# A searched order of steps, loads, casts and copies replaced by another: one q/k group exchanged by DMA, four in quadrants, ten casts on VectorE and not 16

## The chip, the cores and the metric

The kernel runs on one core of a Trainium2 chip. The metric is device time in microseconds (us) of one execution; lower is better. Engines are named as in the profile: PE (TensorE), ACT (ScalarE), DVE (VectorE), POOL (GpSimd), and SP (SyncE), which issues nearly all DMAs.

## What is computed

Sigmoid attention over 8 batches, 12 heads, 448 positions and head size 64, followed by a token-mixing MLP whose mixing weights are computed from its own input. All inputs and the output are float32.

```python
def _attn_ref(q, k, v):
    S = q.shape[2]
    scale = 1.0 / np.sqrt(q.shape[-1])
    scores = scale * np.matmul(q, k.transpose(0, 1, 3, 2)) - np.log(S)
    attn = 1.0 / (1.0 + np.exp(-scores))
    return np.matmul(attn, v).astype(np.float32)

def _moe_ref(x, w_q, w_k, w_out):
    d_hyper = w_q.shape[1]
    wq = x @ w_q
    wk = x @ w_k
    scale = 1.0 / np.sqrt(d_hyper)
    W_tok = scale * np.einsum('bsd,btd->bst', wq, wk)
    mixed = np.einsum('bst,btd->bsd', W_tok, x)
    return (np.maximum(mixed, 0.0) @ w_out).astype(np.float32)
```

Between the two, the heads are put side by side: x is 8 x 448 x 768. There is no softmax, so no row sums: each score goes through a sigmoid by itself. The mixing is done as wq times (wk transposed times x), so that the 448 x 448 matrix W_tok is never built.

## The kernel before

**Groups.** Four heads of one batch are a group; there are 24 groups, three to a batch (a batch is called a unit, u). Each group has seven blocks of 64 keys. q, k and v of a group are loaded as float32 by one DMA each (`load1`, 448 KB) into one of six buffers `ld`, cast to bf16 (`cast1`), and q and k are brought into the tile `qk` with the head size on the partitions (`tr`). `scores` multiplies one block of keys with all queries of four heads: four 64x64 matmuls (L303), then one sigmoid over 128x896 on ACT (L308). `values` (L321) adds up seven blocks of attention times v; after the seventh, the sum is copied to `xt` (L330).

**MLP of a unit.** x is turned around by `tr_x` (L344 in whole 128x128 blocks, L361 in 64x64), and projected by `mlp_wqk` (L400, or L387 in four 64x64 tiles, whose two halves are then added at L394 and L395). `mlp_wkn` turns wk, `mlp_tmp` (L431) or `mlp_tmp_tiled` (L447, L451, L452) makes wk times x, and `mlp_mix` (L471, L483) multiplies with wq, with the relu in the eviction (L457 on ACT, L459 on DVE). The output product of two units together (a window w) is `out_pair` (L516), `out_halves` (L556) or `out_chunk` (L600), with evictions at L525, L561, L562 and L633 and stores issued by SP.

**How q and k are turned** differs from group to group, by the letter of the group in PLAN:

- q/k: a plain cast, 28 transposes of 64x64 each on PE (L212) into PSUM, and one copy to `qk` (L291). a/b: the same with 7 transposes of 128x128 (L220, L286).
- c/d: a cast that also rearranges (L188), six copies of 32 partitions on POOL (`arrange`: L157, L160, L163), and two DVE transposes in blocks of 32x32 (L259), one by c and one by d. Nothing of it is on PE.
- r, s, z: the rearranging cast, two DVE transposes by r (L252), and `quadrants` on DVE (L228): two of 32 partitions by s, two by z. No `arrange`.
- e, f, g: the rearranging cast; e and f each make two DVE transposes, one into `qk` and one into the tile `mv`; g (`move`) has SP issue four DMAs which copy quarters of `mv` over quarters of `qk`. No `arrange`. Before uses no e, f, g.

**The order is a string.** `PLAN` has one letter for each piece of work, and the loop over PLAN at L812 issues it: S a score step, P a values step, W or L one of the six projection steps of a unit (W in one matmul, L in four tiles), x or X or Y one transposition of a third of x (x in 64x64 blocks), N, U or T, M and O or I the later MLP steps, C two DMAs that copy rows of w_out to other partitions, F and E matmuls on zeros that compute nothing. A lower-case p, o, m, i, l, t, u or y puts the eviction that the step ends with on ACT instead of DVE; only the step that ends a sum has one. All engines get their instructions in the order of PLAN, and each engine runs its own in that order, with semaphores where it needs another's result.

**Loads and casts** follow `ORDER`. SP issues loads in this order; a load waits until the buffer used six loads before it has been cast (`pump_loads`). A name without a dot is cast on POOL, one with a dot on DVE (`cast_one`), at the first score step that is at least nine steps behind its load. So a cast that is late holds back the load six places later, and everything behind that on SP.

PSUM is eight banks in four pairs: a score step, an open sum, a transposition each hold a pair or half of one until evicted.

Of the kernel before, what the change touches and what calls it, by code (L numbers as in the profile page):

```python
# [17 lines left out]
def kernel(  # L18
# [101 lines left out]
    def xt(u, j):  # L120
# [4 lines left out]


    PLAN = (
        "SSSFFFFKSqSFFSSkFFSPPSFPpSPPPSSSqkPPPSPPSpPSaSbSPPPSSXPSPPSr"
        "XSPSSsWWSSzWWWXSPWSppPSPNPPSqSkSUSXSMSpppSPMSppPSqkSPSPpPSXS"
        "PpPSWWSWcWSMSXdSWWPSPPSpNPpSPqSkSSUxSMSppSPPpSpPSoOSMCSooqSk"  # L130
        "SOOCMSpPPScpppSPSodOSSoXSSOLLLSLcLLSppPSPppPSSdoOSOSCxNCScOS"
        "USdPrSPpPSPpPpspSpPpSpSoPSXoSMzSooSLLLxSLLLSpPPSpPPScPSOXSSd"
        "OooSpCMpSPppPSPSoNMSCYOxSppPSPSocoPdSpPSoOSxScUdSLLLSLLLSppp"
        "cPSPPPSoOSdMSoOSXSMSprPPSppPSPoSoSoomszxoOcSOSOSoOSdNoSOSUSP"
        "pSMpPPppPPPSSPpcdLLLLSLLppooxmmoOScooSSoOOSONSoSOPdpSPPpSpoS"
        "POSOoSToSOoSOPSPPcSPPpPomMOmoxOSLLSLLdLLSooSoSOSoOScNoSOPSPp"
        "SPPPSoodSPoSOSoSOxSOSxoPppSTSppPpPpPPmpppmmWWWWYWWyIxNIiitii"
        "IMiIMmIIiOOoOooOOooOOoOoo"
    )
    PLAN = "".join(PLAN)  # L140
    KIND = ["a"] + [t for t in PLAN if t in "qacer"]
# [540 lines left out]
    for n in range(7):  # L682
# [1 line left out]


    ORDER = (
# [5 lines left out]
    )  # L692
    BY = {"s": [], "v": []}
    for x in ORDER.split():
# [219 lines left out]
```

## Time and profile before

| | |
|---|---|
| three runs | 187.12 us median (186.6 to 187.13) |
| the profiled execution | 188.48 us, of which the span from first to last instruction 186.7 |
| sigmoids on ACT (L308) | 168, the first at 6.2 us, the last at 162.1; 926 ns each in the mean, 141.2 us busy in all |
| granted PE clock | 0.995 in the mean |
| DMA | 48.52 MB, mean 260 GB/s |
| copies within SBUF (w_out) | 12 DMAs of 96 KB, 5.6 to 8.4 us from issue to landing, median 7.1 |

The sigmoids are the clock of the kernel: 0.8 us from one to the next where nothing holds them up, one for each S in PLAN. Matmuls are pipelined: a row's mean (357 ns at L303) is the time of one from start to end, and four of them take 0.19 us of the engine where they follow one another. A row of the timeline gives start, duration, engine, line, operation and tiles, the number of instructions merged into it, and in brackets how long the engine was idle before it and what ended that.

### The profile page before, as it was taken

Reading aid. Unit: us, or ns where it says so; the run is one execution under the profiler, and the core shown is the slowest. Engines: PE = TensorE matmul, PEld = TensorE weight load, DVE = VectorE, ACT = ScalarE, POOL = GpSimd, SP = SyncE. Lnnn points to the kernel's source line nnn. Section 1 sums busy time; section 2 is a strip of 40 time slices with the busy share of each in tenths; the row PEclk is TensorE's granted clock in tenths of the full one; section 3 lists DMA queues with packets and bytes.
Section 4 is the critical chain, followed back from the end, with each engine's and each line's share of the span. In section 5 each row is a group of like instructions: output and inputs, shape, how many; then the busy total and the mean of one; then the engine's idle time right before and its main releaser. Section 6 shows DMA issues by size and latency. Waiting matters only on the chain.

```text
span 186.7 us, 8457 instructions
## 1 busy us (share of the span) xinstructions
PE 175.0 (94%) x3612; PEld 116.9 (63%) x3612; DVE 139.3 (75%) x222; ACT 163.8 (88%) x208; POOL 113.5 (61%) x158
## 2 busy tenths in 40 slices
PE   7798998998799999999999999999999999999990
PEld 7344545553455554655565768778888888869660
DVE  3334697798778989998899899976476865697830
ACT  4799999998979999999999999998998899976320
POOL 1458788994759999799977796997059800000000
PEclk9999999999999999999999999999999999999997
DMA  5999999998989999799999797886677353421596
GB/s 169 366 384 379 322 374 362 346 320 283 353 303 307 311 364 329 244 272 356 375 325 320 235 301 285 255 271 215 165 191 230 86 135 89 115 61 41 141 241 176
DMA packets 26086, 48.52 MB, mean 260 GB/s; under 512 B 3968, under 2 KB 19968, under 8 KB 26048
## 3 DMA queue, kind: packets, MB, share of 16 engines
q1 hardware_dynamic: 25888, 47.79, 79.2%
q8 instruction: 28, 0.46, 1.0%
q10 hardware_dynamic: 160, 0.20, 0.4%
q14 instruction: 10, 0.08, 0.2%
HBM read 35.78 MB, written 11.01 MB: 251 GB/s over the span
## 4 chain that ended last, share of the span: by engine, by line
PE 67%; ACT 11%; DVE 5%; DMA 5%; issue 5%; POOL 3%; SPq 1%; DVEq 0%; ACTq 0%; POOLq 0%
PE banks L516 15%; PE banks L303 13%; PE banks L321 12%; PE banks L600 11%; ACT at L308 10%; DMA ld<-in_q_dram 3%; PE banks L556 3%; PE banks L387 2%; DMA ld<-in_v_dram 2%; PE banks L431 2%; PE banks L344 2%; PE banks L471 2%; DVE qk L228 1%; PE banks L361 1%; DVE xn L349 1%
## 5 line engine op out<-in xcount | busy, mean ns | idle before, releaser
L308 ACT ACTIVATE at<-banks 128x896 bf16<-128x896 f32 x168 | 141.2, 926 | 5.3 <-PE banks L303 4.5
L303 PE MATMUL banks<-qk 64*64 64x448 bf16 x672 | 63.9, 357 | 1.4 <-ACT at L308 0.3
L321 PE MATMUL banks<-at,v 64*64 64x448 bf16 x672 | 46.4, 351 | 0.4 <-ACT at L308 0.2
L303 PEld LDWEIGHTS <-qk 64*64 64x64 bf16 x672 | 26.5, 105 | 18.2 <-issue 8.7
L516 PE MATMUL banks<-wout,mx 64*64 64x384 bf16 x672 | 35.9, 323 | 0.3 <-issue 0.3
L321 PEld LDWEIGHTS <-v 64*64 64x64 bf16 x672 | 24.1, 106 | 9.7 <-issue 3.7
L330 DVE CAST xt<-banks 128x896 bf16<-128x896 f32 x20 | 21.7, 1087 | 8.3 <-PE banks L321 8.0
L188 POOL CAST qk<-ld 128x896 bf16<-128x896 f32 x21 | 25.2, 1213 | 4.3 <-issue 1.4
L516 PEld LDWEIGHTS <-mx 64*64 64x64 bf16 x672 | 24.5, 107 | 4.1 <-issue 0.7
L600 PE MATMUL banks<-wout,mx 128*128 128x384 bf16 (+1 forms) x138 | 24.7, 320 | 0.1
L198 POOL CAST v<-ld 128x896 bf16<-128x896 f32 x23 | 21.6, 949 | 2.4 <-DMA ld<-in_v_dram 1.6
L157 POOL COPY swap<-qk 32x448 uint32<-32x448 uint32 x26 | 15.1, 582 | 11.4 <-DVE qk L188 10.0
L459 DVE TENSOR_SCALAR mx<-banks 128x1024 bf16<-128x1024 f32 (+2 forms) x19 | 18.6, 989 | 2.3 <-PE banks L483 0.9
L600 PEld LDWEIGHTS <-mx 128*128 128x128 bf16 x138 | 12.0, 97 | 11.3 <-issue 5.0
L163 POOL COPY qk<-swap 32x448 uint32<-32x448 uint32 x26 | 15.6, 600 | 1.5
L259 DVE STREAM_TRANSPOSE qk<-qk 128x448 f32<-128x448 f32 x26 | 16.3, 631 | 0.0
L525 DVE COPY o<-banks 128x768 f32<-128x768 f32 x11 | 10.5, 957 | 7.0 <-PE banks L516 5.2
L160 POOL COPY qk<-qk 32x448 uint32<-32x448 uint32 x26 | 14.5, 556 | 1.5
L374 DVE COPY xn<-banks 128x1024 bf16<-128x1024 bf16 (+1 forms) x12 | 7.7, 645 | 2.3 <-PE banks L361 1.9
L457 ACT ACTIVATE mx<-banks 128x448 bf16<-128x448 f32 (+1 forms) x11 | 8.0, 768 | 1.4 <-PE banks L483 0.8
L349 DVE COPY xn<-banks 128x1024 bf16<-128x1024 bf16 (+1 forms) x11 | 7.3, 660 | 2.1 <-PE banks L344 1.3
L188 DVE CAST qk<-ld 128x896 bf16<-128x896 f32 x11 | 7.9, 750 | 0.1
(95 smaller groups left out, 210.7 us busy)
## 6 DMA issues: line engine op xcount, KB each, us to landing
ld<-in_q_dram SPq DMA_DIRECT2D x24, 448.0 KB, 6.1
ld<-in_v_dram SPq DMA_DIRECT2D x24, 448.0 KB, 6.1
ld<-in_k_dram SPq DMA_DIRECT2D x23, 448.0 KB, 5.8
out_dram<-o SPq DMA_DIRECT2D x42, 192.0 KB, 4.0
ld<-in_moe_w_out_dram SPq DMA_DIRECT2D x6, 384.0 KB, 5.9
out_dram<-ld SPq DMA_DIRECT2D x11, 192.0 KB, 2.8
wout<-wout SPq DMA_DIRECT2D x12, 96.0 KB, 7.1
out_dram<-ld SPq DMA_DIRECT2D x4, 96.0 KB, 2.5
```

Source lines behind the costliest of these rows:

```text
L157: eng.tensor_copy(out=z[lo], in_=w[hi, 0])
L163: eng.tensor_copy(out=w[lo, 1], in_=z[lo])
L188: COPY[e](out=f[:, :, "qk".index(nm)].rearrange("p e i d y -> p e y i d"), in_=ld.pop((nm, n)).rearrange("p (y i e d) -> p e y i d", y=2, ...
L198: COPY[e](out=t16.rearrange("p i b d -> p b i d"), in_=ld.pop((nm, n)).rearrange("p b (i d) -> p b i d", i=NI),)
L259: nc.vector.transpose(out=qk[n][:, t].rearrange("p t i n -> p (t i n)").bitcast(F32), in_=w)
L303: nc.tensor.matmul(sc[HALF[h], g, 0:S], qk[n][HALF[g], h, 1, i, :], qk[n][HALF[g], h, 0].rearrange("p i n -> p (i n)"), start=True, stop=True,
L308: nc.scalar.activation(at, sc[:, :, 0:S], ACTF.Sigmoid, bias=attn_bias, scale=attn_scale)
L321: nc.tensor.matmul(ps[HALF[g], h, 0:S], ld["v16", n][HALF[h], i, g, :], ats[n, i][HALF[h], g, :], start=(i == 0), stop=(i == NI - 1),)
L330: COPY[eng](out=xt(u, j)[:, :, 0:S], in_=ps[:, :, 0:S])
L459: nc.vector.tensor_scalar(dst, ps, moe_scale, 0.0, ALU.mult, ALU.max)
L516: nc.tensor.matmul(ps[HALF[x], y, 0:NB], mx[HALF[y], u, b, 64 * (i - 3 * y) : 64 * (i - 3 * y) + 64], wout16[HALF[y], slot(y, b), x * NB : ...
L600: nc.tensor.matmul(ps, mxs[w][:, 2 * S * c + m * P : 2 * S * c + (m + 1) * P], wout16[:, c, w0:w1], start=(c == 0), stop=(c == NC - 1),)
```

## The change

Only the two strings change; every letter in the new ones is already served by the code.

```diff
     PLAN = (
-        "SSSFFFFKSqSFFSSkFFSPPSFPpSPPPSSSqkPPPSPPSpPSaSbSPPPSSXPSPPSr"
-        "XSPSSsWWSSzWWWXSPWSppPSPNPPSqSkSUSXSMSpppSPMSppPSqkSPSPpPSXS"
-        "PpPSWWSWcWSMSXdSWWPSPPSpNPpSPqSkSSUxSMSppSPPpSpPSoOSMCSooqSk"
-        "SOOCMSpPPScpppSPSodOSSoXSSOLLLSLcLLSppPSPppPSSdoOSOSCxNCScOS"
-        "USdPrSPpPSPpPpspSpPpSpSoPSXoSMzSooSLLLxSLLLSpPPSpPPScPSOXSSd"
-        "OooSpCMpSPppPSPSoNMSCYOxSppPSPSocoPdSpPSoOSxScUdSLLLSLLLSppp"
-        "cPSPPPSoOSdMSoOSXSMSprPPSppPSPoSoSoomszxoOcSOSOSoOSdNoSOSUSP"
-        "pSMpPPppPPPSSPpcdLLLLSLLppooxmmoOScooSSoOOSONSoSOPdpSPPpSpoS"
-        "POSOoSToSOoSOPSPPcSPPpPomMOmoxOSLLSLLdLLSooSoSOSoOScNoSOPSPp"
-        "SPPPSoodSPoSOSoSOxSOSxoPppSTSppPpPpPPmpppmmWWWWYWWyIxNIiitii"
-        "IMiIMmIIiOOoOooOOooOOoOoo"
+        "SSSFFFFKESqSSFFjSFFSpSPPpSPPqSPSSkppSPSpPPSPSabSXSrESpSPpppS"
+        "XpPSSSSsWXWWWSpWSzWPSpPpSNPPSSSabSUSXSMSSPppqkSPPSPPPSPPSpMp"
+        "SpSPSWXcSSWWWWWSdPpppNSMSPSPPSFXSxSqkSUSppSMPPSPPPSOoMSSOOSq"
+        "kSooSPPrSMPCpPSpPCSooSsSSozXOLSLLLSLLCcPSPppSPPPSOSdOSOSCNxS"
+        "cOSUSPppSSdprpPPsPpSpPPSPSOPSXoSMSOoLCSLzxCSLLLLSppPSPppcSPS"
+        "odXSSoOOSMSppppSpcPPSONxSMYOSdSpppSPoopSpPSOOSxScUdSLLLSLLLS"
+        "pPPcSpPPSPoSodSMoSOSXmMPpSppSrPpOSosPSoPoozoSxSOOSOcSONSOdOS"
+        "SUpSPPPeSMpppllfllPPSpPllpSpOPgOSNOOSSOoxSoOSOSOmMOtopScPppp"
+        "SSPPoomodOSSoOSPOSOpSPPPSpPmOOSMOSOLLSLcdLSLoLSoSoOSSoONcoxd"
+        "SopPxPSPPPSPOSOxSoSoTOSOSoSOPpPSPPxSpppPpmpmpPPLmLLxLLLyiiiN"
+        "IIuiIMiMimIIIOoOOooOOOoOoOooo"
     )
...
     ORDER = (
-        "q1 .k1 v0 v1 q2 k2 k3 q3 v2 q4 k4 w0 v3 q5 v4 q6 k5 q7 w5 k6 v5 "
-        "q8 k7 .w4 .k8 k9 v6 w3 v7 .q9 q10 v8 w6 .k10 w2 w1 q11 .v9 v10 "
-        "k11 .k12 .q12 v11 .q13 k13 v12 v13 q14 v14 k14 v15 q15 k15 .q16 "
-        "v16 k16 .k17 .q17 q18 v17 v18 q19 k18 k19 k20 .k21 v19 .k22 q20 "
-        ".k23 q21 .q22 v20 q23 v21 v22 v23 "
+        "q1 .k1 v0 q2 k2 v1 k3 q3 v2 k4 q4 w0 v3 q5 .q6 k5 q7 v4 k6 w2 "
+        ".k7 v5 v6 w5 .w6 k8 w3 q8 k9 q9 v7 v8 w1 w4 v9 k10 q10 k11 q11 "
+        "v10 q12 k12 .k13 q13 v11 v12 q14 k14 q15 v13 .q16 k15 v14 v15 "
+        "v16 k16 .k17 .q17 k18 k19 v17 q18 q19 q20 k20 k21 v18 k22 .k23 "
+        "q21 v19 v20 .q22 v21 q23 v22 v23 "
     )
```

Counted out, by what the letters issue:

- Group 5 is turned by a/b, not q/k. Group 10 by r, s, z, not c/d. Group 20 by e, f, g, not c/d. All others stay as they were (r, s, z: 4, 13, 18; c/d: 7, 11, 12, 14 to 17, 19, 21 to 23).
- 25 rearranging casts on POOL, not 21; 36 plain casts of q, k and v, not 34; six of w in both. On DVE seven rearranging casts, not 11; two plain, not four; one of w in both (w6, not w4).
- 11 `arrange` on POOL, not 13, six copies each.
- The last unit's projection in four tiles (L), not one (W); its U in the untiled form. One x in 64x64 blocks more, one whole less.
- Before the last score step ACT has two evictions of `out_chunk` more, one of `out_pair` more, one each of the partial sums at L394 and L451 more, one of `mlp_mix` less, one of `values` less. Behind it two values steps less and one x less on PE.
- Two E added; nine F in both, one of them now near step 52.

The rest is where each letter stands. The counts of S, P, W and L together, x, N, U, M and O are the same.

More of the change, by code (lines that the diff above doesn't have):

```diff
@@ L127 @@
     PLAN = (
-        "SSSFFFFKSqSFFSSkFFSPPSFPpSPPPSSSqkPPPSPPSpPSaSbSPPPSSXPSPPSr"
-        "XSPSSsWWSSzWWWXSPWSppPSPNPPSqSkSUSXSMSpppSPMSppPSqkSPSPpPSXS"
-        "PpPSWWSWcWSMSXdSWWPSPPSpNPpSPqSkSSUxSMSppSPPpSpPSoOSMCSooqSk"
-        "SOOCMSpPPScpppSPSodOSSoXSSOLLLSLcLLSppPSPppPSSdoOSOSCxNCScOS"
-        "USdPrSPpPSPpPpspSpPpSpSoPSXoSMzSooSLLLxSLLLSpPPSpPPScPSOXSSd"
-        "OooSpCMpSPppPSPSoNMSCYOxSppPSPSocoPdSpPSoOSxScUdSLLLSLLLSppp"
-        "cPSPPPSoOSdMSoOSXSMSprPPSppPSPoSoSoomszxoOcSOSOSoOSdNoSOSUSP"
-        "pSMpPPppPPPSSPpcdLLLLSLLppooxmmoOScooSSoOOSONSoSOPdpSPPpSpoS"
-        "POSOoSToSOoSOPSPPcSPPpPomMOmoxOSLLSLLdLLSooSoSOSoOScNoSOPSPp"
-        "SPPPSoodSPoSOSoSOxSOSxoPppSTSppPpPpPPmpppmmWWWWYWWyIxNIiitii"
-        "IMiIMmIIiOOoOooOOooOOoOoo"
+        "SSSFFFFKESqSSFFjSFFSpSPPpSPPqSPSSkppSPSpPPSPSabSXSrESpSPpppS"
[3 more added lines that the diff above has]
+        "cOSUSPppSSdprpPPsPpSpPPSPSOPSXoSMSOoLCSLzxCSLLLLSppPSPppcSPS"
+        "odXSSoOOSMSppppSpcPPSONxSMYOSdSpppSPoopSpPSOOSxScUSdLLLSLLLS"
+        "pPPcSpPPSPoSodSMoSOSXmMPpSppSrPpOSosSPoSoozoSxSOOSOcSONSOdOS"
+        "SUpSPPPeSMpppllfllPPSpPllpSpOPgOSNOOSSOoxSoOSOSOmMOtopScPppp"
+        "SSPPoomodOSSoOSPOSOpSPPPSpPmOOSMOSOLLSLcdLSLoLSoSoOSSoONcoxd"
+        "SopPxPSPPPSPOSOxSoSoTOSOSoSOPpPSPPxSpppPpmpmpPPLmLLxLLLyiiiN"
+        "IIuiIMiMimIIIOoOOooOOOoOoOooo"
     )
```

## The prediction

> I count score steps: step n is the n-th S of PLAN, its matmuls at L303 and its sigmoid at L308; group g needs its q and k at step 7g+1.
>
> **What bounds the kernel now.** First the page's busy line, then the stretches of the span up to step 63, from there to the last sigmoid, and the rest.
>
> ```profile
> span 186.7 us, 8457 instructions
> PE 175.0 (94%) x3612; PEld 116.9 (63%) x3612; DVE 139.3 (75%) x222; ACT 163.8 (88%) x208; POOL 113.5 (61%) x158
> ...
> 0.00:61.00 61.00, 54.23 (x1056) 30.40 (x1060) 41.97 (x76) 54.99 (x69) 42.66 (x59) 1.00 0.94 328
> 61.00:162.00 101.00, 100.52 (x2200) 71.42 (x2196) 82.02 (x119) 98.01 (x119) 70.87 (x100) 1.00 0.80 250
> 162.00:187.00 25.00, 20.24 (x368) 15.11 (x358) 15.32 (x30) 10.74 (x22) 0.00 (x0) 0.96 0.51 128
> ```
>
> The columns are PE, PEld, DVE, ACT, POOL, then clock, DMA share and GB/s. To 61 us the DMA engines are full (0.94) and ACT sets the pace. From 61 to 162 us PE (100.5 of 101.0) and ACT (98.0) are both full: what either gets more of there moves the last step. After 162 us PE alone works. Next, ACT's waits in the first two stretches, and the end of the chain of waits:
>
> ```profile
> ACT at L308 <- PE banks L303: 2.7, 5, 1.0
> ...
> ACT at L308 <- PE banks L303: 2.1, 7, 0.4
> ...
> 174.57 7.85 PE banks L600 x53
> 182.45 0.37 DVE ld L630
> ```
>
> The sigmoids waited 2.7 us for scores before 61 us and 2.1 after; the chain ends in matmuls. So I judge each moved piece by three questions: does it add to ACT or PE before step 168, does it shorten PE after it, does it make a score step wait?
>
> **Work moved within the saturated pair.** I counted the letters of both PLANs by what each issues. Before step 168, ACT gets two more copies of output chunks (0.49 each, L633), one of an output pair (0.83, L525), one of a partial sum in each of W and U (0.48 each, L451), and loses one mix eviction (1.04, L457) and one values eviction (0.92, L330): 0.98 + 0.83 + 0.96 - 1.96 = +0.8 us. PE gets two more P steps (the chain shows two in 0.38, so 0.19 each) and one tiled x (0.38) there: +0.8 as well. These lie side by side, so the last step comes 0.8 us later, not 1.6. After step 168 PE has two P less (-0.38), one whole x less (-0.55, "PE banks L344 x8"), and U by 8 matmuls in place of 14 (0.77 for 0.64, +0.13): -0.8 us. The last unit's six W go from one matmul to four tiled ones: 4.8/18 against 7.7/30 us a step, the same. Its new add (L395) and GpSimd copy (L396), 0.6 each, lie under an x and three output parts, 0.38 + 3 x 0.49 = 1.8 us of PE; without that cover they cost 1.2. The sum of this part is zero.
>
> **Quadrants.** Group 10 goes from c (six GpSimd copies, 3.5 us, and two transposes) to r: the same two transposes and four of quadrants. These lines of VectorE and PE show what that costs, from group 4 and from where group 10 will be:
>
> ```profile
> 26.01 2.64 DVE L228 STREAM_TRANSPOSE qk<-qk 32x448 f32<-32x448 f32 x4
> 28.69 0.31 PEld L303 LDWEIGHTS <-qk 64*64 64x64 bf16 x4 [0.20 <-DVE qk L228]
> ...
> 61.00 11.71 ACT L308 ACTIVATE at<-banks 128x896 bf16<-128x896 f32 x14 [0.22 <-PE banks L303]
> ...
> 60.96 1.08 DVE L459 TENSOR_SCALAR mx<-banks 128x896 bf16<-128x896 f32 x1
> 61.95 0.64 DVE L259 STREAM_TRANSPOSE qk<-qk 128x448 f32<-128x448 f32 x1
> 62.84 1.09 DVE L330 CAST xt<-banks 128x896 bf16<-128x896 f32 x1 [0.25 <-ACT at L308]
> ```
>
> A pair of quadrants takes 1.3 us, and even now group 4's last pair ended just as step 29 wanted it. In the new order the second pair of group 10 is issued one step before step 71. Set in these rows: the values eviction of group 8 ends near 64.4 (62.84 + 1.09, pushed back 0.5 by the mix eviction, which now comes after step 65), then two pairs, 2 x 1.3, to 67.0. Step 71's matmuls now run near 65.7 and its sigmoid starts at 66.83, inside that unbroken run of 14; matmuls from 67.0 (0.4 us) give 67.4. I take +0.6; between 0, if the sigmoids are late by then anyway, and 1.3, a whole pair.
>
> Group 4's second pair now follows an xn copy (0.69) which waits for transposes after step 26. That step's matmuls start at 26.12; with a W and an x, the transposes end near 27.25, the copy at 28.1, the pair at 29.4, the sigmoid at 29.85 in place of 29.48. I take +0.4; between 0 and 0.8.
>
> **Casts.** VectorE loses ten (w4, k8, q9, k10, v9, k12, q12, q13, k21, k22) and gets four (q6, k7, w6, k13). GpSimd gets six more, four rearranged (1.21) and two plain (0.95), 6.7 us, and loses twelve copies of arranging (0.58), 7.0: it ends with the same load, and it is 30% idle between 61 and 162 us, which hides it. The gain can come where VectorE's casts now stand in front of something:
>
> ```profile
> 40.48 1.34 DVE L198 CAST k<-ld 128x896 bf16<-128x896 f32 x1
> 41.29 1.32 POOL L198 CAST v<-ld 128x896 bf16<-128x896 f32 x1
> 41.74 0.67 DVE L349 COPY xn<-banks 128x1024 bf16<-128x1024 bf16 x1
> ...
> 43.43 3.35 ACT L308 ACTIVATE at<-banks 128x896 bf16<-128x896 f32 x4 [0.47 <-PE banks L303]
> ```
>
> Casts of w4 and k8 held up an xn copy, that a W, that step 44: 0.47 us of idle ACT. Two casts (k7, w6) still stand in that place, with the W a step later; I take half, -0.25, between -0.47 and 0. VectorE's cast took 1.34 us beside GpSimd's, and 0.61 elsewhere (q9, 47.11). [...]
>
> **Loads.** The order changes which cast frees which of the six buffers. The load of k7 now waits for q6's cast on VectorE behind step 29, near 30.7 us, where the 21st load was issued at 27.14; DMA then stands idle about 1 us. The 27th waits for k7's cast, near 38.4 in place of 34.39. The slack of k7 hides this (its first transpose ran at 43.34); without it 1 us. By the 31st load both orders are level (before issued it at 41.85, w6's cast frees it near 42).
>
> **Group 20 by DMA.** Two more VectorE transposes of 0.63 each, no copies by GpSimd, four transfers on SP's queue. They stand behind v21's load, which waits for k22's cast on GpSimd; behind them on SP are stores only. From step 132: mix eviction 1.2, two transposes 1.3, the cast 1.2, the load and four issues 0.4 each, 2.0, with 0.6 for PE: issued at +6.3. PE has 13.4 us of steps between 132 and 141. The nearest transfers within SBUF land 5.6 to 8.4 us after issue, so at +11.9 to +14.7, with the median of 7.1 just at +13.4. I take 0; the far end is 1.3 late. [...]
>
> **Other edits** (at nothing): group 5 by whole transposes costs PE 0.3 where ACT paces; two E fill PE waits at the start; an F at step 52 costs 0.3 if the scores there are short of PE.
>
> **Sum.** 0.8 - 0.8 + 0.6 + 0.4 - 0.25 = +0.75: span 186.7 to 187.45. That execution took 188.48 with what lies around the span, above the median of the runs, 187.12; on the median's scale I forecast 187.9.
>
> **Rivals.**
> The forecast, a little slower by waits at steps 29 and 71: 0.42.
> *Faster*: in the saturated stretch, before has eleven PE steps between the scores at 125.2 us and twelve between those at 142.7 (3.95 and 3.54 us from sigmoid to sigmoid); the new order has nine at most. If ACT's waits there, 2.1 us for scores and 0.7 for mixes, halve (-1.4), VectorE's casts give all of -0.47, and the quadrant waits halve (+0.5): 185.8. It decides once ACT waits under 1.5 us there. Against it: PE stays full, and its work is not less. 0.30.
> *Nothing*: sigmoids are late enough for the quadrants to be ready, 187.1: 0.16.
> *Group 20 late*: transfers at the slow end, 1.3 us on step 141 on top of the forecast, 189.2: 0.12; for it, 7.1 us to land; against, few loads are in flight by then.
>
> **From these the numbers.** 0.3% of 187.12 is 0.56 us, about what can be told from no change. Slower by more: most of the forecast (0.38) and group 20, 0.50. Within: the neutral case and bits of two others, 0.20. Faster: 0.30. The range reaches into the faster rival and over the last: 185.6 to 189.5; the likeliest case alone 187.3 to 188.6.
>
> **What would show it.** In the changed profile: step 71 waits for L228 (0.4 us or more); step 29 too; ACT 0.8 more busy before its last sigmoid, PE's time from there to its last matmul 0.8 shorter; no wait of L303 for a DMA into qk near step 141. I am wrong if the last sigmoid starts before 162 us, or if step 71 has no wait.

## The result, and the profile after

The changed kernel is slower: 188.85 us in the median (187.72 to 189.75, four runs) against 186.87 (186.6 to 187.13, four runs), a ratio of 1.0117 (95%: 1.0074 to 1.0159). Measured once more with more runs it was 189.23 against 186.79: 1.0132 (1.0096 to 1.0169). The ratios leave out the executions of a kernel that took over 1.5% longer than its fastest.

Its profiled execution, at 187.72 us, is the shortest of its own four, and the one of before, at 188.48, is longer than any of the four of before. So these two traces, 185.9 us against 186.7, show the opposite of the medians, and the difference has to be looked for in more than this pair. From the page of the profiled execution after, the busy line and the line of the queue q8, of kind instruction, to which the experiments come back:

```profile
span 185.9 us, 8441 instructions
PE 174.8 (94%) x3612; PEld 117.3 (63%) x3614; DVE 138.0 (74%) x217; ACT 163.3 (88%) x211; POOL 112.4 (60%) x153
...
q8 instruction: 28, 0.46, 1.0%
```

The same three stretches (columns PE, PEld, DVE, ACT, POOL, clock, DMA share, GB/s):

```profile
0.00:61.00 61.00, 55.58 (x1052) 32.88 (x1055) 42.16 (x75) 56.56 (x71) 42.92 (x59) 1.00 0.97 335
61.00:162.00 101.00, 100.12 (x2218) 71.17 (x2213) 82.89 (x118) 96.60 (x121) 68.92 (x94) 1.00 0.79 249
162.00:187.00 25.00, 19.12 (x358) 13.28 (x353) 12.96 (x26) 10.12 (x21) 0.56 (x1) 0.93 0.48 128
```

ACT's waits for scores, in the first stretch and in the second:

```profile
ACT at L308 <- PE banks L303: 1.0, 2, 0.5
...
ACT at L308 <- PE banks L303: 3.8, 9, 1.0
```

Before 61 us they fell from 2.7 to 1.0 us: the new beginning is better. After 61 us they rose from 2.1 to 3.8. The end of the chain of waits is of the same kind as before, one long run of output matmuls (start, duration, what):

```profile
173.20 6.95 PE banks L600 x42
...
180.17 0.49 ACT ld L633
```

The two waits for quadrants that I forecast did not come. VectorE around step 29 and around step 71, from the timeline of after:

```profile
25.99 0.64 DVE L228 STREAM_TRANSPOSE qk<-qk 32x448 f32<-32x448 f32 x1
26.66 0.69 DVE L349 COPY xn<-banks 128x1024 bf16<-128x1024 bf16 x1
27.39 1.30 DVE L228 STREAM_TRANSPOSE qk<-qk 32x448 f32<-32x448 f32 x2
...
60.21 1.09 DVE L459 TENSOR_SCALAR mx<-banks 128x896 bf16<-128x896 f32 x1 [0.24 <-PE banks L483]
61.27 1.09 DVE L330 CAST xt<-banks 128x896 bf16<-128x896 f32 x1
62.40 2.64 DVE L228 STREAM_TRANSPOSE qk<-qk 32x448 f32<-32x448 f32 x4
```

and ACT's sigmoids at the same places:

```profile
27.53 3.41 ACT L308 ACTIVATE at<-banks 128x896 bf16<-128x896 f32 x4
...
63.11 5.80 ACT L308 ACTIVATE at<-banks 128x896 bf16<-128x896 f32 x7
```

Step 29's sigmoid started at 29.22 and step 71's at 65.56, each inside an unbroken run: the quadrants ended at 28.69 and 65.04, before they were wanted. What does stand out after 61 us is this, on the weight loads of TensorE:

```profile
153.24 0.13 PEld L303 LDWEIGHTS <-qk 64*64 64x64 bf16 x2
154.49 0.11 PEld L303 LDWEIGHTS <-qk 64*64 64x64 bf16 x2 [1.12 <-issue]
```

A score step has four loads. Here two ran, then TensorE stood still for 1.12 us, and then the other two ran, though all four belong to the same step and read the same tile. "issue" says that the profile shows nothing that it waited for. The experiments are about such gaps.

### The profile page after: what moved, and what is told of

Its sections match the earlier page's. It is cut to its first block, busy times and chain, and to the rows that moved or that the text cites. A ratio compares the mean times of both kernels' runs of the same rounds, so it can differ in the third digit from the quotient of the medians.

```text
span 185.9 us, 8441 instructions
## 1 busy us (share of the span) xinstructions
PE 174.8 (94%) x3612; PEld 117.3 (63%) x3614; DVE 138.0 (74%) x217; ACT 163.3 (88%) x211; POOL 112.4 (60%) x153
## 4 chain that ended last, share of the span: by engine, by line
PE 77%; ACT 13%; DVE 4%; issue 3%; ACTq 0%; DVEq 0%
PE banks L303 16%; PE banks L516 15%; PE banks L321 13%; ACT at L308 12%; PE banks L600 12%; PE banks L387 4%; PE banks L556 3%; PE banks L431 2%; PE banks L361 2%; PE banks L344 2%; PE banks L677 2%; DVE xt L330 2%; PE banks L471 2%; PE banks L483 1%; PE banks L400 1%
## 5 line engine op out<-in xcount | busy, mean ns | idle before, releaser
L303 PE MATMUL banks<-qk 64*64 64x448 bf16 x672 | 62.3, 358 | 3.6 <-ACT at L308 1.8
L321 PE MATMUL banks<-at,v 64*64 64x448 bf16 x672 | 47.7, 351 | 0.3 <-ACT at L308 0.2
L188 POOL CAST qk<-ld 128x896 bf16<-128x896 f32 x25 | 29.4, 1193 | 12.0 <-issue 6.5
L157 POOL COPY swap<-qk 32x448 uint32<-32x448 uint32 x22 | 12.4, 565 | 7.7 <-DVE qk L188 6.4
L160 POOL COPY qk<-qk 32x448 uint32<-32x448 uint32 x22 | 13.2, 601 | 1.3
L396 POOL COPY wq<-wqk 64x448 bf16<-64x448 bf16 x6 | 3.7, 612 | 16.4 <-DVE wqk L395 16.1
L163 POOL COPY qk<-swap 32x448 uint32<-32x448 uint32 x22 | 12.1, 552 | 1.3
L374 DVE COPY xn<-banks 128x1024 bf16<-128x1024 bf16 (+1 forms) x13 | 8.4, 648 | 3.0 <-PE banks L361 2.6
L228 DVE STREAM_TRANSPOSE qk<-qk 32x448 f32<-32x448 f32 x16 | 10.2, 636 | 0.4
L387 PE MATMUL banks<-xt,wqk 64*64 64x448 bf16 x144 | 10.1, 351 | 0.0
```

Source lines behind the costliest of these rows:

```text
L160: eng.tensor_copy(out=w[hi, 0], in_=w[lo, 1])
L188: COPY[e](out=f[:, :, "qk".index(nm)].rearrange("p e i d y -> p e y i d"), in_=ld.pop((nm, n)).rearrange("p (y i e d) -> p e y i d", y=2, ...
L303: nc.tensor.matmul(sc[HALF[h], g, 0:S], qk[n][HALF[g], h, 1, i, :], qk[n][HALF[g], h, 0].rearrange("p i n -> p (i n)"), start=True, stop=True,
L321: nc.tensor.matmul(ps[HALF[g], h, 0:S], ld["v16", n][HALF[h], i, g, :], ats[n, i][HALF[h], g, :], start=(i == 0), stop=(i == NI - 1),)
L387: nc.tensor.matmul(ps[HALF[x], y, 0:S], wqk16[HALF[y], c, 64 * x : 64 * x + 64], xt(u, c // 2)[HALF[y], c % 2, 0:S], start=(c == 0), stop= ...
```

## The experiments

Each ran in five rounds beside runs of before. Steps are counted by sigmoids, as in the prediction.

**Which part of the order costs?** First the changed kernel again, then three kernels that take one part of the new strings and the rest from before. They are joined near steps 85, 130 and 167, where both PLANs have issued the same counts of every kind (but for the z and g of groups 10 and 20).

```diff
 h1: PLAN = NEW[:264] + OLD[261:]                ORDER = NEW[:57] + OLD[57:]
 m1: PLAN = OLD[:261] + NEW[264:423] + OLD[420:] ORDER = OLD[:57] + NEW[57:71] + OLD[71:]
 e1: PLAN = OLD[:420] + NEW[423:]                ORDER = OLD[:71] + NEW[71:]
```

> The changed kernel once more, beside the one before. Ratio 1.012 (1.008 to 1.016) if the four runs so far stand for it, near 189 us. Its profiled execution was the shortest of the four (span 185.9) while that of before (188.48 us) was longer than all its timed ones, so the two traces do not show the difference of the medians. If single executions differ by chance waits, this profile's span will lie nearer 187, with waits of ACT for scores that the first one did not have.

> The new order of steps up to score step 85 and of the first 57 loads, the old order behind them: the same work at the joint, so only the first 77 us are new, with group 10 in quadrants. Quadrants theory (the prediction): the waits at steps 29 and 71 make up the loss, +1.0 us or more here, ratio 1.005 to 1.010, and the two other parts nothing. Theory that the loss is at the end: 1.000. Theory of chance waits everywhere: about 1.004.

> The new order from score step 85 to 130 and of loads 58 to 71 alone. Quadrants theory: 1.000. Theory that the loss is at the end: 1.000. Theory of chance waits everywhere: about 1.004. Here the rest of the order is that of before.

> The new order from score step 130 on alone: group 20 by DMA, and the new tail. Quadrants theory: 1.000, since ACT's 0.8 us more and PE's 0.8 us less behind step 168 cancel. Theory that the loss is at the end (the exchange by DMA, or more waiting between PE and ACT): 1.008 to 1.012, with the wait to be seen in front of step 141 or between 141 and 168. Chance waits everywhere: about 1.004.

Measured, ratios to before: a1 1.0132 (1.0096 to 1.0169), h1 1.0127 (1.0074 to 1.018), m1 1.0108 (1.0078 to 1.0138), e1 1.0037 (0.9993 to 1.0082). The parts add to 2.7% and the whole is 1.3%, so this cut names no part. m1 has none of the new quadrants and is as slow as the rest, but two of the joints turned out to bring waits of their own. In m1, TensorE waits for a cast of v that GpSimd comes to late:

```profile
124.26 0.57 PE L321 MATMUL banks<-at,v 64*64 64x448 bf16 x8 [1.08 <-POOL v L198]
```

And the kernels with the new head and the old rest need 26.75 to 26.79 us from step 85 to 113 where before needs 25.89, each with one gap of 0.75 us at L431. So these three kernels say little of the change. The profile of a1 (187.90 us, span 186.1, not the 187 that I had expected) again lies near the shortest of its kernel.

**What the gaps have in common.** I numbered TensorE's weight loads and matmuls together, in order of start. After 61 us, the profiles of all the kernels of this study together have 21 gaps of over 0.4 us in the weight loads for which no releaser is shown. Eighteen stand at number 194 + 256k (within 4; a record missing from a trace moves the count by 2); the other three are the one place L431 of the joint just named. Before 61 us the mark "issue" tells less: six to eight gaps of 0.4 to 0.7 us stand there at the same instructions in nearly every profile of an order, wherever its blocks end, while the gap at L431 near 51 us is there only when a block ends at it. Each of the eighteen ends 2.2 to 3.1 us after a packet of 16384 B on the queue q8, of kind instruction, of which every kernel has some 28: 16384/256 is 64 B. In the profile after there are 28 for 7226 loads and matmuls, one for every 258, and a3 (below), with 256 more of them, has 29. This reads as TensorE's program coming in blocks of 256 instructions, and a block being used up before the next is there. The next kernels test it by moving the block ends against the order, with nothing but the warm-up at the start changed (b2 as shown; a2, and a3 further below, in the changed kernel, with 21 and 67 matmuls and with 6 and 154):

```diff
-    for _ in range(32):
+    for _ in range(19):
         nc.tensor.matmul(pairs[3][:, 0, 0:P], zeros[:, 0:P], zeros[:, 0:P], start=True, stop=True)
+    for x in range(77):
+        g, h = x % 2, x // 2 % 2
+        nc.tensor.matmul(pairs[3][HALF[h], g, 0:64], zeros[HALF[g], 0:64], zeros[HALF[g], 0:64], start=True, stop=True)
```

> The kernel before, run against itself, for a profile nearer to its usual time than the one at hand (span 186.7, where most of its executions have 184.0 to 185.3) and for what the comparison gives when nothing is changed. Two theories are now open. Fetch: counted over TensorE's loads and matmuls together, the stalls of 0.4 to 1.1 us for which the profile shows no releaser stand at number 194 + 256k (1730, 3010, 4802 before; 6082 after; 4290, 5570 in others), each 2.2 to 3.1 us after a packet of 16384 B on the instruction queue q8, which is 256 instructions of 64 B: TensorE has used up a block of its program before the next one is there. Order: the new order itself costs 2 us by many small waits on data. Fetch expects: ratio 1.000 within 0.003; a profile of 184 to 185.5 us whose TensorE gaps over 0.24 us at the block ends add to under 1.2 us (1.9 in the slow one). Order expects: the same ratio; the gaps at block ends add to as much as in the slow one, and the time is gained elsewhere.

> Before, with the warm-up of TensorE at the start made of 96 matmuls in place of 32 in about the same time (19 of 128 columns and 77 small ones, 3.3 us), so 128 instructions more: every later block of 256 instructions ends half a block earlier in the order, nothing else changes. From the stretches between block ends in the profiles (4.1 to 4.6 us where TensorE is densest) and the measured delays of the instruction packets, my estimate of the waits at block ends is 1.3 us for before and 2.4 with this shift. Fetch expects: slower by 1.1 us, ratio 1.006 (1.003 to 1.009), with unexplained stalls at 194 + 256k again, now at other lines. Order expects: 1.000 within 0.002, since the order is that of before.

> The changed kernel, shifted in the same way by 112 instructions (21 matmuls of 128 columns and 67 small ones). The estimate of its waits at block ends is 1.8 to 2.6 us unshifted, most of all the block that ends at step 55 (0.8 to 1.1 alone), and 0.9 to 1.2 us with this shift, the least of all shifts tried in steps of 16. Fetch expects: faster than the unshifted one by 0.9 to 1.4 us, ratio to before 1.006 (1.003 to 1.009) in place of 1.0125, no stall near step 55. Order expects: 1.0125 within 0.003, as unshifted.

Measured: b0 0.9997 (0.9968 to 1.0027), with a profiled span of 185.2; b2 1.0083 (1.0049 to 1.0118); a2 1.0043 (1.0003 to 1.0082). The order of before, made to end its blocks elsewhere, lost 0.8%, as the fetch theory said and not as the order theory did. Part of this may be the warm-up's own: in the profile of b2 the first sigmoid starts at 6.73 us, in the five with the warm-up and the beginning of before at 6.12 to 6.54. That the new order gained is not shown: the interval of a2 lies below that of the unshifted kernel (1.0096 to 1.0169), but it rests on nine of its twelve executions, and the median of all twelve is 189.13 us, against 189.23 for a1; the executions of before beside a2 were slower than those beside a1 (187.55 against 186.79). What the traces do show is that the gaps moved with the blocks. Before, in its first profile and in b0, had one at step 54 in U's matmuls; in b2 that one is gone, and another stands in the values matmuls of step 57. One line of each (before, b0, b2, then a2, whose largest gap stands at step 155), from the weight loads of the timelines:

```profile
51.58 0.11 PEld L431 LDWEIGHTS <-wkn 128*64 128x64 bf16 x2 [1.08 <-issue]
```

```profile
51.10 0.11 PEld L431 LDWEIGHTS <-wkn 128*64 128x64 bf16 x2 [0.65 <-issue]
```

```profile
54.47 0.14 PEld L321 LDWEIGHTS <-v 64*64 64x64 bf16 x6 [0.83 <-issue]
```

```profile
149.25 0.11 PEld L516 LDWEIGHTS <-mx 64*64 64x64 bf16 x2 [1.32 <-issue]
```

The first two are the same instruction in two executions of one program, and the gap is 1.08 in one and 0.65 in the other; the two of 0.72 and 0.56 us that the first profile of before has at 87.2 and 129.1 us are below 0.4 in b0. The last line shows how rough the estimate behind the shift was: this one block took 1.32 us, where the estimate had 0.9 to 1.2 for all of them together.

**A control for the shift, and two attempts at a faster kernel.** A shift by 256 moves no block end; and the new head, shifted, should have been faster than before.

> Control for the edit that shifts: the changed kernel with 256 instructions more in the warm-up (6 matmuls of 128 columns, 154 small ones), a whole block, so that every later block ends where it ends unshifted, while the warm-up is changed more than in the other two. Fetch expects the time of the unshifted changed kernel: ratio 1.0125 (1.009 to 1.016), stalls again at 194 + 256k, near step 55 among them. Rival, warm-up: the 112 helped because small matmuls make a better warm-up; then this one is at 1.004 or below.

> h1 (new steps to step 85, then the old order), shifted by 112 instructions. Unshifted it measured 1.0127. Taking the least time of each stretch over all executions of the same order, the new order needs 52.3 us to step 57 (6.4 + 22.8 + 23.1), the old 53.2 (6.2 + 23.3 + 23.8); the rest is the old one's. My estimate of the waits at block ends is 2.1 us unshifted and 0.9 with this shift, where before has 1.2. Fetch expects: 1.2 us less than before, ratio 0.994 (0.990 to 0.998). Order expects: 1.0127, as unshifted.

> The same with the changed kernel's steps after step 167 too (its last stretch 24.1 us in place of 24.5, least times). Fetch expects: 1.6 us less than before, ratio 0.991 (0.987 to 0.996), faster than both kernels. Order expects: no faster than before.

Measured: a3 1.0086 (1.0049 to 1.0122), h2 1.0064 (1.0025 to 1.0102), ht 1.009 (1.0053 to 1.0128). The control came out a little under what was expected, with an interval that reaches into it, and it rules out the warm-up (1.004 or below); but it overlaps that of a2, and the medians of all executions are alike (189.12 and 189.13 us), so this pair does not show that the shift by 112 helps. In its profile the gaps stand at block ends again, behind sigmoids 138, 157 and 160 (not at step 55, as I had expected; at step 50 there are 0.35 us, but the score step after it has 0.34 without a block end). The last two lines below are one score step cut in two, as in the profile after:

```profile
129.07 0.43 PEld L516 LDWEIGHTS <-mx 64*64 64x64 bf16 x12 [1.16 <-issue]
...
154.16 0.13 PEld L303 LDWEIGHTS <-qk 64*64 64x64 bf16 x2
155.22 0.11 PEld L303 LDWEIGHTS <-qk 64*64 64x64 bf16 x2 [0.93 <-issue]
```

h2 and ht are misses: slower than before, not faster. I had summed the best times of stretches and overlooked that the joint near step 85 costs 0.86 us (the 26.75 above), and each had late blocks (a gap of 0.86 us in h2, two of 0.8 in ht), where the estimate had 0.9 us for all of them. That h2 is better than h1 (1.0064 against 1.0127) has the sign that the theory wants; the intervals overlap.

**Why is a block late?** Over 392 blocks of the fourteen profiles of this study, the table sets the time from the first instruction of a block to the start of the packet for the next one against the busy share of the DMA engines in the first 2 us of it:

```
DMA share    blocks   packet after the block's begin, us: mean, middle 80%
under 0.3      45     0.60   -0.05 to 1.12
0.3 to 0.8     91     0.83    0.16 to 1.57
0.8 to 0.95    84     2.03    0.96 to 3.47
over 0.95     172     2.60    1.70 to 3.50
```

And nowhere did a new block begin sooner than 2.18 us after its packet's start. So a block of 256 instructions waits when TensorE gets through the one before it in less than the packet's delay plus some 2.2 us: where the matmuls are short (many blocks after 117 us take only 4.2 to 4.8 us) and DMA is full (over 0.95, 2.60 + 2.2 = 4.8 us in the mean). Two kernels change the DMA load and no instruction of TensorE: x1 adds loads that nobody reads to before, x2 shortens the stores of the changed kernel (x1 also declares its four tiles; x2 cuts the stores of `out_chunk` before the last score step in the same way).

```diff
 x1 (before), behind each S
+            if 144 <= c <= 164 and c % 2 == 0:
+                n = c // 2 % 4
+                nc.sync.dma_start(out=extra[n], in_=moe_w_out[n * P : (n + 1) * P, :])
 x2 (after)
-            nc.sync.dma_start(out=dst, in_=o[HALF[x]])
+            nc.sync.dma_start(out=dst[0:8], in_=o[HALF[x]][0:8])
```

> Before with eleven loads more, of 384 KB each, into tiles that nothing reads, one behind every second score step from 145 to 165: DMA traffic and nothing else. Over 251 block ends of nine profiles the instruction packet came 0.6 us after the block before began where DMA was under 0.3 busy, 1.9 at 0.8 to 0.95 and 2.7 (0.9 to 4.5) above 0.95, and no instruction of a new block ran sooner than 2.18 us after its packet started. Here blocks last 4.4 to 5.4 us and DMA is 0.47 busy between 148 and 162 us, so packets come 0.85 after and nothing waits. Fetch expects packets 1.9 to 2.7 us after, waits of 0.15 to 0.6 a block, 1 to 2.4 us in all, ratio 1.005 to 1.013, and TensorE's gaps at 194 + 256k. Order (waits for data alone) expects nothing, 1.000 within 0.003, or, if the stores get late by the traffic, waits of ACT or VectorE for tiles of o that the profile shows as such.

> The changed kernel, whose output stores before the last score step write 8 rows of each 64 only: the rest of those outputs is left out, with the same instructions and waits and fewer bytes. Fetch expects packets sooner between 62 and 162 us (under 1 us after the block's begin in place of 1.1 to 1.9), the stalls at steps 138 and 157 to 160 gone (2.2 us in the profile a3, 0.6 to 1.3 in the other three of this order), those near steps 50 to 55 as before: 0.8 to 1.8 us faster than the changed kernel, ratio 1.006 (1.002 to 1.008). Order expects 1.0125 within 0.003, since no engine waited for a store.

Measured: x1 1.0041 (1.0003 to 1.0078), x2 1.0012 (0.9978 to 1.0046). The windows from 148 to 162 us, of x1 and of x2 (x1 first; before has there a DMA share of 0.47 in b0, the changed kernel 0.47 in a3):

```profile
148.00:162.00 14.00, 13.80 (x368) 11.15 (x360) 7.05 (x11) 13.32 (x17) 0.56 (x1) 1.00 0.94 286
```

```profile
148.00:162.00 14.00, 14.00 (x434) 11.49 (x430) 8.82 (x14) 13.20 (x17) 2.63 (x4) 1.00 0.10 17
```

In x1 the packets of the blocks that begin at 144 to 159 us came 2.3 to 3.1 us after the block's begin, not 0.5 to 1.5 as in b0, and from step 141 to the end each stretch grew: 15.73 to 15.92, 5.96 to 6.24, 5.54 to 5.82, 24.58 to 24.89, 1.1 us in all. Of this 0.8 lie before the end of TensorE's last matmul; the other 0.25 come after it, while the last stores land, and are not a late block. The largest gap of x1 after 61 us, at a block end (its line numbers are one higher):

```profile
149.21 0.27 PEld L517 LDWEIGHTS <-mx 64*64 64x64 bf16 x8 [0.54 <-issue]
```

The ratio lies just under the expected 1.005, with an interval that reaches well into it; it rests on eight of twelve executions, and the medians of all of them (188.50 against 187.31) give 1.006. In x2 the packets came 0.8 us after the block's begin in the mean from 62 to 162 us, where the profile after has 1.6, and 0.5 from 144 us on, where that has 1.9. The score step that is cut in two in after and in a3 is whole:

```profile
153.64 0.14 PEld L303 LDWEIGHTS <-qk 64*64 64x64 bf16 x4
153.80 0.49 PEld L516 LDWEIGHTS <-mx 64*64 64x64 bf16 x12
```

With that its time went back to that of before (187.48 against 187.31 us): more than expected (1.002 to 1.008), and wholly outside the intervals of the unshifted changed kernel and of a3. No gap of over 0.4 us without a releaser is left after 61 us. Before with short stores was not tried; it would be expected to lose its own smaller gaps too, so x2 alone does not show how much of the difference between the two orders is late blocks.

## Why the prediction was right in its sign and wrong in its reasons

The sign and the range held: slower, 188.85 where 187.9 was forecast and 185.6 to 189.5 allowed. The reasons did not, so that the number fell into the range is luck: about 1 us of forecast waits did not come, and a loss of about 2 us, for which the sum had no term, took their place. From step 57 on, one order takes the same time in a stretch in several executions, mostly to 0.01 us (steps 57 to 85 in before, b0 and x1: 24.14 each). So I take the least time of each stretch over all profiles of an order (before, b0, b2; after, a1, a2, a3, x2) for what the order itself needs:

```
from sigmoid to sigmoid to 1  1-29  29-57  57-85 85-113 113-127 127-141 141-155 155-162 162-168 to the end   sum
before, least          6.16  23.32  23.76  24.14  25.89   13.57   15.82   15.73    5.96    5.53     24.54  184.42
after, least           6.38  22.82  23.05  24.43  26.05   13.30   16.79   13.86    7.34    5.90     24.12  184.04
b0 (span 185.2)        6.19  23.34  24.35  24.14  25.89   13.63   15.82   15.73    5.96    5.54     24.58  185.16
a3 (span 187.0)        6.38  22.92  23.10  24.54  26.06   13.30   17.88   13.86    8.59    5.90     24.53  187.05
```

By these sums the new order without late blocks would be 0.4 us shorter, not 0.75 longer. These least times were not all reached in one execution, and the 7.34 was reached in x2 alone: the four profiles with whole stores have 8.07 to 8.78 there, which is 7.2 to 7.7 when their gaps of over 0.4 us are taken off. With 8.07 in its place the new order would be 0.35 longer than before. b0 and a3 are the two profiled executions that lie near the medians of their kernels (186.95 for 187.08, 188.83 for 189.12). Over their least sums b0 lost 0.7 us, 0.59 of it at the gap at 51.1; a3 lost 3.0, of which 1.09 at step 138 and 1.25 at steps 157 to 160. So, counted this way, 1.75 of the 1.9 us between them are blocks that came late; the order's gain of 0.4 and a longer end (0.4) about cancel. That is the step that failed: the sum had no term for TensorE's program, though the page of before showed the queue q8 and a share of "issue", and the trace the 1.08 us at L431 shown above.

Point by point:

- **What bounds the kernel**: holds. TensorE full after 61 us (busy 100.5 of 101.0 us before, 100.1 after) is why a block that comes late there mostly goes into the time: before has a gap of 0.56 us at 129.06 us, and the stretch around it is 0.59 longer than in b0. It need not: the 0.54 of x1 at 149.21 made its stretch 0.19 longer.
- **Work moved within the saturated pair** (+0.8 before step 168, -0.8 after): the middle, steps 57 to 168, is 1.0 longer by least times (107.67 for 106.64). TensorE's busy time up to the last sigmoid rose by 0.6 (154.89 to 155.49); ACT's did not rise (153.15 to 152.95). After it TensorE has 0.77 less to do, as counted, but the stretch is shorter by 0.4 only: that term was right as work and twice too large as time.
- **Quadrants** (+0.6 and +0.4): zero each. At step 29 the xn copy started at 26.66, where I had it wait until 27.4, so the second pair ended at 28.69 and not 29.4. At step 71 the mix eviction stood in front, as forecast, but it and the values eviction were done at 62.36, 3.2 us before the sigmoid and not the 2.4 (64.4 for 66.83) that I had; the four ran through in 2.64 us and ended 0.5 before it. "I am wrong if the last sigmoid starts before 162 us, or if step 71 has no wait": both came about (161.79).
- **Casts and loads** (-0.25 and 0): the stretch to step 57 is 1.0 shorter by least times, 52.25 for 53.24, and ACT's waits there fell by 1.7 us, more than the 0.47 that I let the casts give. Which of the casts, the E dummies and the loads gave it, no run here tells.
- **Group 20 by DMA** (0, or 1.3 late): its transfers of 56 KB landed 3.2 us after issue in the median (3.5 to 4.5 in a1, a3 and e1), not 7.1, and no score step waited at 133 us. My figure was that of copies of 96 KB, issued from 56.6 to 95.7 us in before; in the profile after, those have a median of 5.0. The rival of 189.2 comes nearest in its number and did not take place. e1, which has these transfers, is the least slow of the parts.
- **The faster rival** asked for ACT's waits after 61 us to fall; they rose, by the late block at 154.5 among others.

Few block ends show a long gap: of 280 after 61 us in the fourteen profiles 18 have one of over 0.4 us. But those take up to 1.32 us.

What stays open: what sets off a packet, and so why one block end is late in one execution and not in the next; and why the first 57 steps differ by up to 1 us between executions of the same code. The lateness is shown to follow DMA load, and the loss of the new order to go with it. That late blocks make up the whole difference between the two orders is worked out from single profiles and not shown: before with short stores was not run, the shift by 112 brought no clear gain, and the share of each block end in the medians is not measured, since a median is a time without a profile.

## What to carry to other kernels

In a kernel whose TensorE is full with many short matmuls, number the loads and matmuls together and look for gaps without a releaser that repeat every 256: 18 of 21 did here, read as blocks of the program that came late, and packets were late here where the DMA engines were full (2.60 us after the begin of the block before, over a share of 0.95, and 0.60 under 0.3). An order tuned to a fraction of a per cent can be tuned to where its blocks end as well (before lost 0.8% when its blocks were shifted), so that before a new order is judged it is worth trying it with several shifts, by a few dummy instructions at the start. And a part of a tuned order set into another tells of its joints first.

## What the hardware showed that I had not expected

- In the fourteen profiles TensorE's program came, as the gaps and the packet counts read, in packets of 16384 B for 256 instructions, one block ahead, and a new block started no sooner than 2.18 us after its packet's start. The packet started 0.60 us after the begin of the block before it where DMA was under 0.3 busy, and 2.60 us after where it was over 0.95 (means).
- Such a gap differs from one execution to the next at the same instruction (1.08 and 0.65 us at L431; 1.12 and 0.66 at step 161 of the changed kernel): a good part of the 2 to 4 us by which runs of one kernel differ here can come from this, though no run separates it.
- Loads that nobody waits for, in a stretch where DMA was half idle (0.47 busy in b0, 0.94 with them), brought the packets 0.9 to 2.6 us later and made the time to TensorE's last matmul 0.8 us longer in the one profile taken.
